# Third-block low parts of groups 0 to 2: VectorE in place of GpSimd, in an attention and two-MoE kernel

## The chip, the cores and the metric

The kernel runs on one NeuronCore of a Trainium2 chip. The metric is the device time of one execution in microseconds (us), the median of several runs. Engines are called by the names of the profile: PE is TensorE's matrix multiply and PEld its weight load, DVE is VectorE, ACT is ScalarE, POOL is GpSimd, SP is the queue that issues the transfers.

## The reference

All arithmetic is on 32-bit floats. Three layers follow one another; the output of each is the input of the next.

```
attention: q, k, v of 2 x 8 heads x 768 tokens x 64; a local band of 16 tokens plus 24 block summaries,
           softmax, product with v; the result is x with 1536 tokens x 512
layer 1:   h = x @ w_in (512 x 2048);  g = h * sigmoid(1.702 h);  x = g @ w_out (2048 x 512)
layer 2:   gate = sigmoid(x @ w_gate);  val = x @ w_val (both 512 x 1536);  out = (gate * val) @ w_out (1536 x 512)
```

## The kernel before, in words

**Products in high and low parts.** PE multiplies numbers of a shorter format (`F32R`). To keep the accuracy of 32 bits, every operand x is split into a high part xH, a rounded copy that ACT makes, and a low part xL = x - xH. A product is then three matmuls that add up in one PSUM bank: low times high, high times low, high times high (`mm3`, line 484, and `product`, line 190). A matmul of 128 x 512 streams 512 columns.

**Blocks and groups.** The 1536 tokens are three blocks (`blk` 0, 1, 2) of 512. The hidden features of a layer are cut into groups `g` of 256 (8 in layer 1, 6 in layer 2), a group into two tiles `f` of 128 features. `first` (line 517) computes the two feature tiles of one group and block: for each, 12 matmuls into a bank `ps_h`, then `gated`. `gated` (line 511) takes the activation with ACT into a tile `sg` and calls `split`. `split` (line 503) makes the high part `gh` with ACT (line 508) and the low part `gl` = `sg` - `gh` with GpSimd (line 509). `second` (line 541) multiplies the two tiles of a group by the group's rows of the output weights: four column pieces `m`, each 6 matmuls into a bank `ps_o`. Of group 0, ACT copies the piece into the accumulator `acc` (line 571); of later groups, DVE adds it (line 575). Within a piece the second matmul is the first to read `gl` of tile 0, and the fifth reads `gl` of tile 1.

**The stretch of the change.** Groups 0 and 1 of blocks 0 and 1 are done during the attention stage. Behind it, `steps` (line 925) lists three steps for the third block: groups 0, 1 and 2 (`PAIRED` is 2). The loop at line 927 gives PE this order: first of group 0, first of group 1, second of group 0, first of group 2, second of group 1. The second of group 2 is spread between the first products of the next phase. `run` (line 910) traces these; after each yield of the main generator it pulls one step of the weight loader (`load`, line 118) and one step of `folding`. From the second step on, `folding` is `input_sums` (line 248): thirteen DVE instructions on 128 x 1024 tiles (line 253), all with two inputs in SBUF, that form the sums and differences of blocks 0 and 1 and their low parts. The paired phase of group 2 onward (`pair`, line 402) needs these sums: it computes two feature tiles of two blocks with 7 products in place of 8. `load` brings one weight matrix piece of 128 x 1024 numbers: the DMA lands 64-bit words in `raw` (two buffers), DVE takes them apart (lines 132 and 150), ACT rescales (line 140) and rounds (line 155), DVE makes the low part (line 157). For some pieces it makes four sums as well (lines 173, 182, 184).

**What sets the order.** Only SP follows the program text by hand. On the other engines the order of instructions is fixed at build time: the framework's scheduler plays the program on a timeline of its own and issues what is ready there, the earlier in the program first. An engine then runs its list in that order, and waits at an instruction whose inputs are not there. `keep_in_program_order` (lines 134 and 254) pins an instruction behind the DVE instruction traced just before it; `behind` (line 111) pins one behind another that is named. Line 153 pins line 150 of group 3's input weights behind the addition of piece 0 of group 1, third block (`added[1, 1, 2, 0]`).

**Buffers.** After the attention stage the feature tiles have 7 buffers `sg` and 5 each of `gh` and `gl`; `ps_f` has four PSUM banks and `ps_s` four.

The lines that the change and the steps of the prediction touch:

```
927    for step in steps:
929        run(first(*step))
932        if prev: ... run(second(*prev, False))
937        if step == (1, 0, 2): folding = sums_1

912    for n, _ in enumerate(main):
913        pull(1)
914        next(folding, None)
```

Of the kernel before, what the change touches and what calls it, by code (L numbers as in the profile page):

```python
# [14 lines left out]
ALU = mybir.AluOpType  # L15
# [14 lines left out]
def attention_moe_moe2_kernel(ctx: ExitStack, tc: tile.TileContext, ins: dict, out: bass.AP):  # L30
    nc = tc.nc
# [186 lines left out]
    PAIRED = 2  # L218
# [123 lines left out]
    def halves(g):  # L342
# [30 lines left out]
        def out(j, f, x):  # L373
            if f not in sg:
                sg[f] = sg_slots.tile([P, TB], F32, "sg")
            to = sg[f][:, (FIRST, SECOND)[j]]
            nc.scalar.activation(to, x[:, FIRST], AF.Sigmoid)
            nc.vector.tensor_tensor(out=to, in0=x[:, SECOND], in1=to, op=ALU.mult)
            done[f] = done.get(f, 0) + 1
            if done[f] == 2:  # L380
                split((2, g, 2, f), sg[f])
# [116 lines left out]
    def gate_by(to, val, sg):  # L498

        nc.vector.tensor_tensor(out=sg, in0=val, in1=sg, op=ALU.mult)  # L500
        split(to, sg)

    def split(to, sg):
        name = "_".join(map(str, to))
        gh = gh_slots.tile([P, TB], F32R, f"gh{name}")
        gl = gl_slots.tile([P, TB], F32R, f"gl{name}")
        gt[to] = gh, gl
        nc.scalar.copy(gh, sg)  # L508
        nc.gpsimd.tensor_tensor(out=gl, in0=sg, in1=gh, op=ALU.subtract)  # L509

    def gated(to, x):

        sg = sg_slots.tile([P, TB], F32, "sg")
        nc.scalar.activation(sg, x, AF.Gelu_apprx_sigmoid)
        split(to, sg)
# [90 lines left out]
    with tc.manual_schedule(engines={mybir.EngineType.SP}), ExitStack() as es:  # L606
# [192 lines left out]
        for _ in range(4):  # L799
# [28 lines left out]
            out=win, in_=win, pattern=[[0, NSLOT], [1, P - W0]], compare_op=ALU.is_gt, fill=NEG,  # L828
# [3 lines left out]
            out=win, in_=win, pattern=[[0, NSLOT], [-1, P - W0]], compare_op=ALU.is_gt, fill=NEG,  # L832
# [225 lines left out]
```

## Time and profile before

| | us |
|---|---|
| median of 3 runs (lowest to highest) | 625.32 (624.49 to 626.36) |
| the profiled execution, its own time | 624.76 |
| its span, first to last instruction | 623.0 |

What lies outside the span is 1.76 us. In the profile, a time such as 137.19 is microseconds from the start of the span. A row of the timeline has start, duration, engine, line, operation, the tiles written and read, their shapes, and in brackets the idle time of the engine before the row with what ended it. Rows of one engine can overlap by a little: the next instruction starts before the last has drained, so the spacing of the starts is what one instruction costs its engine. The busy shares of the whole execution are 96% for PE, 71% for DVE, 51% for ACT and 33% for POOL. The granted clock of TensorE is 1.00 at 2.4 GHz and 0.50 at 1.2 GHz.

### The profile page before, as it was taken

The numbers are of one execution on the slowest core, as the hardware profiler recorded it, in microseconds if no ns is written. First come the engines' busy times: TensorE is split into PE (matmuls) and PEld (weight loads), VectorE is DVE, ScalarE is ACT, GpSimd is POOL, SyncE is SP. The second block draws the span as 40 slices with busy tenths as digits, with TensorE's granted clock in tenths as the row PEclk, the third lists the DMA queues.
The fourth block names the chain that finished last, engine by engine and source line by source line (L and its number), as shares of the span: only waits on it lengthen the run. The fifth ranks groups of instructions, "written<-read, shape, count | busy, mean of one in ns | idle before, by whom it ended". The sixth has DMA issues, their size and how long they took to land.

```text
span 623.0 us, 8772 instructions
## 1 busy us (share of the span) xinstructions
PE 600.9 (96%) x3342; PEld 499.3 (80%) x3342; DVE 445.2 (71%) x662; ACT 316.1 (51%) x624; POOL 205.4 (33%) x164
## 2 busy tenths in 40 slices
PE   7798999986999999999999999999999999999997
PEld 4576887765888888888888888888898888898896
DVE  6799666492799875975559889677778668777434
ACT  4688657572465444545345567635345245344230
POOL 6796676255133222321332131021121222112030
PEclk9999999996999999999999999999999999999999
DMA  9998742012044121230202003412211212100014
GB/s 314 344 308 284 250 121 66 1 68 67 1 135 136 69 67 68 68 108 28 68 0 69 0 2 135 135 68 67 70 68 68 67 68 69 68 1 0 1 46 157
DMA packets 25161, 58.10 MB, mean 93 GB/s; under 512 B 1568, under 2 KB 1824, under 8 KB 25120
## 3 DMA queue, kind: packets, MB, share of 16 engines
q1 hardware_dynamic: 24400, 56.24, 27.8%
q10 hardware_dynamic: 720, 1.31, 0.6%
q8 instruction: 26, 0.43, 0.3%
q14 instruction: 15, 0.12, 0.1%
HBM read 53.08 MB, written 3.15 MB: 90 GB/s over the span
## 4 chain that ended last, share of the span: by engine, by line
PE 87%; DMA 8%; POOL 3%; DVE 2%; issue 0%; ACT 0%; SPq 0%; ACTq 0%; POOLq 0%
PE ps_o L489 37%; PE ps_y L197 16%; PE ps_x L197 11%; PE ps_v L197 11%; PE ps_h L197 4%; PE ps_h L489 4%; DMA xH<-in_moe_w_out 3%; DMA k<-in_k 3%; POOL gl L509 2%; DMA vt<-in_vt 2%; PE ps_s L710 2%; PE ps_x L762 1%; PE ps_p L743 1%; DMA q<-in_q 1%; PE ps_s L708 0%
## 5 line engine op out<-in xcount | busy, mean ns | idle before, releaser
L509 POOL TENSOR_TENSOR gl<-sg,gh 128x512 fp32r<-128x512 f32 x84 | 131.8, 1576 | 380.2 <-ACT gh L508 279.8
L575 DVE TENSOR_TENSOR acc<-ps_o,acc 128x512 f32<-128x512 f32 x143 | 96.4, 684 | 71.8 <-PE ps_o L489 71.7
L489 PE MATMUL ps_o<-gl,w_1H 128*128 128x512 f32 x192 | 76.3, 399 | 7.8 <-POOL gl L509 7.8
L489 PE MATMUL ps_o<-gh,w_1H 128*128 128x512 f32 x192 | 75.5, 394 | 0.0
L489 PE MATMUL ps_o<-gh,w_1L 128*128 128x512 f32 x192 | 72.3, 401 | 1.5 <-ACT gh L508 1.4
L508 ACT CAST gh<-sg 128x512 fp32r<-128x512 f32 x84 | 51.5, 621 | 33.6 <-DVE sg L500 25.1
L489 PE MATMUL ps_o<-w_2L,gh 128*128 128x512 f32 (+1 forms) x146 | 56.6, 388 | 0.0
L489 PE MATMUL ps_o<-w_2H,gh 128*128 128x512 f32 (+1 forms) x146 | 56.4, 386 | 0.0
L489 PE MATMUL ps_o<-w_2H,gl 128*128 128x512 f32 (+1 forms) x146 | 56.3, 389 | 0.1
L150 DVE SCALAR_TENSOR_TENSOR da<-da,db 128x1024 uint32<-128x1024 uint32 x34 | 46.2, 1358 | 9.9 <-ACT da L140 9.2
L489 PEld LDWEIGHTS ps_o<-gl,w_1H 128*128 128x128 f32 x192 | 36.7, 191 | 15.8 <-POOL gl L509 8.4
L140 ACT ACTIVATE da<-da 128x1024 f32<-128x1024 f32 x34 | 36.1, 1061 | 20.8 <-DVE da L132 18.8
L489 PEld LDWEIGHTS ps_o<-gh,w_1L 128*128 128x128 f32 x192 | 36.5, 191 | 9.6 <-ACT gh L508 2.0
L489 PEld LDWEIGHTS ps_o<-gh,w_1H 128*128 128x128 f32 x192 | 36.6, 191 | 7.5
L723 ACT ACTIVATE e<-ps_s,nm 128x128 f32<-128x128 f32 x96 | 34.2, 377 | 9.4 <-DVE nm L715 8.3
L699 POOL TENSOR_SCALAR kx<-k 128x384 f32<-128x384 f32 x24 | 32.0, 1335 | 19.1 <-DMA k<-in_k 8.5
L489 PEld LDWEIGHTS ps_o<-w_2H,gh 128*128 128x128 f32 x146 | 27.4, 188 | 5.7
L489 PEld LDWEIGHTS ps_o<-w_2H,gl 128*128 128x128 f32 x146 | 27.4, 188 | 5.2 <-DVE acc L575 0.3
L489 PEld LDWEIGHTS ps_o<-w_2L,gh 128*128 128x128 f32 x146 | 27.5, 188 | 5.0
L710 PE MATMUL ps_s<-kx,q 128*128 128x128 f32 x192 | 28.5, 296 | 3.1 <-POOL kx L699 1.7
L710 PEld LDWEIGHTS ps_s<-kx,q 128*128 128x128 f32 x192 | 25.8, 205 | 6.7 <-POOL kx L699 3.2
L132 DVE TENSOR_SCALAR db<-raw 128x1024 uint32<-128x1024 uint32 x33 | 28.9, 877 | 0.5
(244 smaller groups left out, 1493.0 us busy)
## 6 DMA issues: line engine op xcount, KB each, us to landing
raw<-in_moe_w_out SPq DMA_DIRECT2D x13, 1024.0 KB, 5.1
raw<-in_moe_w_in SPq DMA_DIRECT2D x8, 1024.0 KB, 7.5
raw<-in_moe_w_gate SPq DMA_DIRECT2D x6, 1024.0 KB, 5.0
raw<-in_moe_w_val SPq DMA_DIRECT2D x6, 1024.0 KB, 5.2
q<-in_q SPq DMA_DIRECT2D x20, 256.0 KB, 9.3
vwin<-in_v SPq DMA_DIRECT2D x6, 768.0 KB, 9.1
k<-in_k SPq DMA_DIRECT2D x8, 400.0 KB, 7.5
out<-acc SPq DMA_DIRECT2D x11, 256.0 KB, 2.0
```

The costliest lines, as they stand in the source:

```text
L132: ins = nc.vector.tensor_scalar(**x)
L140: nc.scalar.activation(af, af, AF.Prelu, scale=REBIAS, alpha=-2.0 ** 32)
L150: ins = nc.vector.scalar_tensor_tensor(out=a, in0=a, scalar=3, in1=b, op0=ALU.logical_shift_left, op1=ALU.bitwise_or)
L197: nc.tensor.matmul(ps, lhsT=a[x][:, kk, :], rhs=b[y][:, kk, :], start=start and i == 0, stop=i == n - 1, skip_group_check=True,)
L489: nc.tensor.matmul(ps, lhsT=a, rhs=b, start=i == 0, stop=i == n - 1)
L508: nc.scalar.copy(gh, sg)
L509: nc.gpsimd.tensor_tensor(out=gl, in0=sg, in1=gh, op=ALU.subtract)
L575: added[layer, g, blk, m] = nc.vector.tensor_tensor(out=a[:, m, :], in0=ps, in1=a[:, m, :], op=ALU.add)
L699: nc.gpsimd.tensor_scalar(out=to, in0=x, scalar1=scale, scalar2=None, op0=ALU.mult)
L710: nc.tensor.matmul(ps[:, j, :], lhsT=t[:, j, :], rhs=kt[:, j, :], start=False, stop=j == G - 1)
L723: nc.scalar.activation(e[:, j, :], s[:, j, :], AF.Exp, bias=nm[:, j:j + 1], accum_out=sm[:, j:j + 1])
L743: nc.tensor.transpose(ps[:, j, :], e[:, j, :], ident)
```

## The change

Of `split`, the low part is computed by DVE and not by GpSimd when the tile is of layer 1, of group 0, 1 or 2, and of the third token block. These are six tiles: two of each group. The other 78 low parts stay with GpSimd.

```
 def split(to, sg):
...
         nc.scalar.copy(gh, sg)
-        nc.gpsimd.tensor_tensor(out=gl, in0=sg, in1=gh, op=ALU.subtract)
+
+        engine = nc.vector if to[0] == 1 and to[1] <= PAIRED and to[2] == 2 else nc.gpsimd
+        engine.tensor_tensor(out=gl, in0=sg, in1=gh, op=ALU.subtract)
```

`to` is (layer, group, block, tile).

## Rows read from the trace of the kernel before

**Rows 1.** The page: the engines, busy time and instructions.

```profile
PE 600.9 (96%) x3342; PEld 499.3 (80%) x3342; DVE 445.2 (71%) x662; ACT 316.1 (51%) x624; POOL 205.4 (33%) x164
```

**Rows 2.** Stretches: busy of PE, PEld, DVE, ACT, POOL; granted clock, DMA share, GB/s.

```profile
137.19:145.07 7.88, 0.39 (x2) 0.00 (x1) 6.71 (x7) 2.72 (x4) 7.88 (x2) 0.67 0.12 42
...
145.07:150.24 5.17, 5.17 (x12) 4.07 (x13) 0.00 (x0) 0.00 (x0) 3.65 (x3) 0.51 0.64 199
...
165.00:175.00 10.00, 10.00 (x46) 8.27 (x45) 9.83 (x14) 5.31 (x8) 1.29 (x1) 1.00 0.08 11
150.24:360.00 209.76, 209.76 (x927) 173.70 (x926) 155.96 (x197) 103.23 (x153) 53.52 (x37) 1.00 0.19 61
360.00:618.00 258.00, 258.00 (x1374) 223.25 (x1373) 181.16 (x257) 117.07 (x185) 51.27 (x35) 1.00 0.19 63
```

**Rows 3.** The waits of PE: engine, line, releaser: us in total, times, longest.

```profile
PE ps_o L489 <- POOL gl L509: 7.8, 2, 7.5
PE ps_s L708 <- ACT e L723: 2.1, 2, 1.2
```

**Rows 4.** The chain that ended last, 126 to 160 us: start, us, what.

```profile
131.90 13.13 POOL gl L509
...
145.07 7.87 PE ps_o L489 x23
152.94 5.44 PE ps_h L489 x24
```

**Rows 5.** The timeline of PE around the wait, and two later starts.

```profile
137.19 0.39 PE L489 MATMUL ps_o<-gh,w_1L 128*128 128x512 f32 x1
145.07 0.79 PE L489 MATMUL ps_o<-gl,w_1H 128*128 128x512 f32 x1 [7.49 <-POOL gl L509]
...
158.21 0.39 PE L489 MATMUL ps_o<-gh,w_1L 128*128 128x512 f32 x1
...
165.24 0.39 PE L489 MATMUL ps_o<-gl,w_1H 128*128 128x512 f32 x1
...
177.03 0.39 PE L197 MATMUL ps_h<-xH,w_0H 128*128 128x512 f32 x1
```

**Rows 6.** The timeline of ACT: the high parts of the six tiles.

```profile
131.20 0.62 ACT L508 CAST gh<-sg 128x512 fp32r<-128x512 f32 x1
...
133.39 0.61 ACT L508 CAST gh<-sg 128x512 fp32r<-128x512 f32 x1
...
138.43 0.62 ACT L508 CAST gh<-sg 128x512 fp32r<-128x512 f32 x1
...
159.10 0.62 ACT L508 CAST gh<-sg 128x512 fp32r<-128x512 f32 x1
```

**Rows 7.** Line 509 in the whole trace: ns shortest, median, longest.

```profile
L509 POOL TENSOR_TENSOR gl<-sg,gh x84: 1262/1295/13118, 56.4 to 612.9; 128x512 fp32r<-128x512 f32 x84
```

**Rows 8.** The timeline of DVE from 131 to 161 us, in part.

```profile
131.79 1.22 DVE L253 TENSOR_TENSOR f<-f,f 128x1024 f32<-128x1024 f32 x1
132.92 0.69 DVE L132 TENSOR_SCALAR db<-raw 128x1024 uint32<-128x1024 uint32 x1
...
143.21 0.69 DVE L132 TENSOR_SCALAR da<-raw 128x1024 f32<-128x1024 f32 x1
159.84 0.69 DVE L575 TENSOR_TENSOR acc<-ps_o,acc 128x512 f32<-128x512 f32 x1 [15.94 <-PE ps_o L489]
160.45 1.71 DVE L150 SCALAR_TENSOR_TENSOR da<-da,db 128x1024 uint32<-128x1024 uint32 x1
...
164.76 1.21 DVE L157 TENSOR_TENSOR w_0L<-da,w_0H 128x1024 fp32r<-128x1024 f32 x1
```

**Rows 9.** The timeline of POOL, 115 to 165 us.

```profile
131.90 16.82 POOL L509 TENSOR_TENSOR gl<-sg,gh 128x512 fp32r<-128x512 f32 x4 [10.88 <-ACT gh L508]
```

**Rows 10.** Line 582: a DVE subtraction with the operands of line 509.

```profile
L582 DVE TENSOR_TENSOR yL<-acc,yH x10: 406/680/1784, 324.5 to 359.7; 128x512 fp32r<-128x512 f32 x8, 128x256 fp32r<-128x256 f32 x2
```

**Rows 11.** The waits of DVE in the whole trace, the longest group.

```profile
DVE acc L575 <- PE ps_o L489: 71.7, 46, 15.9
```

## The prediction

> **What bounds the kernel now.** I read the page first: PE is busy for 96% of the span [rows 1]. The stretches say where: from 150.24 to 618 us PE is busy in every microsecond, at a granted clock of 1.00 [rows 2]. So from there on nothing but PE's own work sets the time, and what starts PE earlier ends the kernel earlier, as long as the other engines keep up. Then I read the waits of PE. They are few: 7.8 us for GpSimd's low part, in 2 waits, one of 7.5, and 2.1 us for the next group [rows 3]. The chain of work shows the one wait in its place: a single low part holds it from 131.90 for 13.13 us, and behind it PE's 23 matmuls take 7.87 us, where the 24 after that take 5.44 [rows 4]. The reader should see two losses: a stop, and slow matmuls after it.
>
> The timeline of PE names the stop. At 137.19 PE starts the second product of group 0, third block; its second matmul is the first to read the low part of tile 0 and starts at 145.07, after 7.49 us of idle time [rows 5]. The stretches show what it does to the clock: 0.67 in the stretch of the idle time, 0.51 from 145.07 to 150.24, that is the lower of the two levels (1.2 of 2.4 GHz), and 1.00 afterwards [rows 2].
>
> Why is a low part of 128 x 512 late by so much? Its high part is done at 131.20 + 0.62 = 131.82 [rows 6], and GpSimd starts 0.08 us later. The median of the 84 low parts is 1.295 us, the shortest 1.262; this one is the longest, 13.118 [rows 7]. Meanwhile DVE runs back to back: from the row at 131.79 to the end of the row at 143.21 its starts follow one another with no idle time in brackets, and then it stands for 15.94 us [rows 8]. DVE's last one ends at 143.21 + 0.69 = 143.90; GpSimd's ends at 131.90 + 13.13 = 145.03, which is 1.13 us later, a little less than one undisturbed low part. The other three, which waited in GpSimd's queue, take (16.82 - 13.13) / 3 = 1.23 us each once DVE stands [rows 4, 9]. So GpSimd got almost nothing done while DVE ran with operands in SBUF, and finished as soon as DVE stopped.
>
> **A rule against this reading.** The Trainium skill, SBUF — State Buffer, Who interferes with whom, says that a DVE instruction with two SBUF inputs and a GpSimd instruction that reads SBUF exclude each other, and that whoever issues first has the ports for that one instruction. By that rule GpSimd would wait for one DVE instruction, to 131.79 + 1.22 = 133.01, and be done at an estimated 134.3; the 7.49 us would have another cause. The trace agrees on the exclusion, and not on its length: the twelve DVE instructions from 131.79 to 143.21 all went first (the first two and the last of them stand in [rows 8]). I go by the trace; the other case is rival B.
>
> **The change, part by part.**
>
> *Removed: six low parts on GpSimd.* Four of them are the row of 16.82 us, two are later ones. Off PE's path but for the first.
>
> *Added: six on DVE.* The nearest row has the same operands, types and 512 columns: 0.68 us median [rows 10]. In a full queue one such instruction costs what lies between two starts, 160.45 - 159.84 = 0.61 us [rows 8], so 6 x 0.61 = 3.7 us of DVE time. DVE's list is fixed at build time, and no row shows the place of the six. They are early in the program, so each should stand about where its high part is done. The early end for tile 0 is 131.82 + 0.68 = 132.5. The late end is the last place ahead of the addition at 159.84, since PE makes that addition's input only after it has read the low part: 143.90 + 0.68 = 144.6. PE wants it at 137.42 (137.19 plus 0.23, the pitch of 5.44 / 24). I take the early end: even two places further, behind the rows at 131.79 and 132.92, it is done at 134.2. Tile 1 has its high part at 133.39 + 0.61 = 134.0 [rows 6] and, one DVE instruction of 1.22 later at worst, is done by 135.9; PE wants it at 137.19 + 4 x 0.23 = 138.1. Group 1's later high part is done at 138.43 + 0.62 = 139.05 [rows 6], and PE comes to group 1's low parts only after 48 more matmuls, past 148.
>
> *The sums behind them.* Four of the low parts push the rest of DVE's run back by 4 x 0.61 = 2.4 us, from 143.90 to 146.3. The cover is the 15.94 us in which DVE stands [rows 8]. It shrinks, as PE comes earlier (below): the addition then starts at 159.84 - 10.1 = 149.7, still 3.4 us behind 146.3. No DMA is issued or moved, and SP's own list stays.
>
> *The pins.* Each input sum is pinned behind the DVE instruction traced just before it. A low part could become that instruction, and the sums would stand behind it. In the code `run` pulls a loader step between the two, and where that step issues nothing on DVE, the addition of `second` has come in between. So I cost the pins at nothing.
>
> *The gain.* From 137.19 to 158.21, the start of the second product of group 1 [rows 5], PE has 48 matmuls: 24 of group 0's second and 24 of group 2's first. At 5.44 / 24 = 0.227 us [rows 4] they take 10.88; they took 21.02. The difference is 10.14 us: 145.07 - 137.19 - 0.23 = 7.65 for the stop and 2.49 for matmuls at the lower clock. I take it that the clock does not fall where PE does not stop: it is 1.00 throughout the 468 us from 150.24 on, in which PE never does [rows 2].
>
> *The last two low parts, and DVE after the gain.* Group 2's second high part is done at 159.72 [rows 6], by 149.6 after the change, and PE wants group 2's low part at 165.24 - 10.14 = 155.1 [rows 5]. Here DVE is nearly full: 9.83 of 10 us from 165 to 175 [rows 2]. The two cost 1.2 us; what GpSimd held up in return, the row at 160.45 with 1.71 against 1.22 for its size [rows 8], is 0.5. The end prices are 0 and +1.2 on PE's path. I take 0: the weights that DVE makes at 164.76 + 1.21 = 165.97 [rows 8] are read by PE at 177.03 at the earliest [rows 5], 11 us later, and all this moves forward with the addition that starts it.
>
> *Sum.* 624.76 - 10.1 + 0 = 614.6 for an execution like the profiled one. The median lies 0.56 above it, so 615.2.
>
> **The rivals.**
>
> *A. Partly given back.* DVE carries 3.7 us more, and in the full stretch after 165 PE has to wait once for a weight piece. Price: 3.7 of idle time and again 2.5 at the lower clock, 6.2 in all, so 621.4. For it: DVE at 9.83 of 10. Against: PE does not wait once from 150 on, and DVE waits for PE 46 times, for 71.7 us [rows 11].
>
> *B. The change does not do what it says.* Not DVE's traffic, but something else that a DVE instruction would meet as well, held the first low part; it then takes as long on DVE. Its end stays near 145.03, the sums behind it still fit ahead of 159.84, and the time is 625.3. Against: the three that follow it take 1.23 us.
>
> *C. Slower: the sums behind a low part that waits for PE.* If DVE's list has group 2's second low part ahead of the row at 131.79, DVE stands until its high part is done, at 149.6 at the best, and the 12.1 us of work up to 143.90 plus 3.7 follow: until 165.4. The first addition, wanted at 149.7, then lets its bank go only at about 166, and PE, out of banks at 154.9, stands for 11 us and pays 2.5 for the clock: 13.5 lost for 10.1 gained, 628.7. It decides as soon as more than about 9 us of that work stand behind. Against: the scheduler lets go ahead what is ready, and this one is ready last.
>
> **How the numbers follow.** The forecast has 0.84, A 0.08, B 0.05, C 0.03. A measurement of this kernel can tell 0.3%, 1.9 us, from no change. B is the same; the forecast and A lie beyond, so faster is 0.91, same 0.06 (B and a mild C), slower 0.03. The forecast's own range is 613.6 (the fastest run shown lies 0.8 below the median, and as much again for other small waits on GpSimd) to 617.0 (the 1.2 us of DVE on PE's path, and part of the clock). I reach up to 618.5, for low parts that stand a few places later, towards A; this leaves out most of A, B and C, under 0.2.
>
> **What would show it.** PE's wait for line 509 is gone from its waits, the row at 145.07 starts at 137.4, and 24 matmuls of that product take about 5.4 us at a clock of 1.00. The six DVE rows of line 509 take 0.68 us; DVE's wait for the addition is some 3 us in place of 15.94. No low part of GpSimd takes over 3 us. It is wrong if PE idles between 137 and 165 or waits for DVE rows later, if the clock still falls there, or if a DVE row of line 509 has idle time before it with sums behind.

## The result, and the profile after

The median of four runs is 615.69 us (615.31 to 616.76); the kernel before has 624.9 in four runs beside them. The ratio is 0.9851, with an interval of 0.983 to 0.9873. The profiled execution is the longest of the four: 616.76 us, span 615.0. The changed lines push the code behind them down by two: line 509 is 511 now, 575 is 577.

The page, the engines (answers to [rows 1]) and the shares of the chain:

```profile
PE 600.4 (98%) x3342; PEld 500.6 (81%) x3342; DVE 447.2 (73%) x668; ACT 316.5 (51%) x624; POOL 188.0 (31%) x158
...
PE 93%; DMA 4%; ACT 1%; DVE 1%; POOL 0%; issue 0%; SPq 0%; POOLq 0%
```

PE's work is what it was (600.9 us before). GpSimd's busy time fell by 17.4 us; the row of 16.82 [rows 9] is gone from it. Line 511 in the whole trace, as in [rows 7]:

```profile
L511 POOL TENSOR_TENSOR gl<-sg,gh x78: 1264/1296/2364, 58.2 to 604.9; 128x512 fp32r<-128x512 f32 x78
...
L511 DVE TENSOR_TENSOR gl<-sg,gh x6: 680/682/695, 135.1 to 153.5; 128x512 fp32r<-128x512 f32 x6
```

The low part of 13.118 us is gone, and no other has taken its place: GpSimd's longest takes 2.364. The waits of PE, the largest three; where [rows 3] had GpSimd's low part with 7.8 us, nothing of line 511 is left:

```profile
PE ps_s L712 <- DMA q<-in_q: 2.4, 2, 2.2
PE ps_s L710 <- ACT e L725: 1.8, 2, 0.9
PE ps_o L489 <- ACT gh L508: 1.7, 1, 1.7
```

All three are in the attention stage. The chain from 126 us on (compare [rows 4]), without the stop and without a slow stretch:

```profile
128.60 10.88 PE ps_h L489 x48
139.48 0.91 PE ps_o L489 x4
...
150.36 5.44 PE ps_o L489 x24
```

The stretches (columns as in [rows 2]) confirm it: the 21.76 us from the first product of the third block to the second product of group 1 are full, at a clock of 1.00.

```profile
128.44:139.32 10.88, 10.88 (x50) 9.01 (x48) 10.88 (x14) 7.57 (x10) 0.00 (x0) 1.00 0.14 44
139.32:150.20 10.88, 10.88 (x50) 9.01 (x48) 9.81 (x11) 7.39 (x11) 0.00 (x0) 1.00 0.18 61
150.20:360.00 209.80, 209.80 (x933) 173.77 (x932) 161.68 (x209) 104.37 (x154) 54.00 (x36) 1.00 0.20 65
```

**Two clocks to read by.** The first matmul of the third block starts at 128.44 here and started at 126.31 before. So every time of after is set against one of before plus 2.13. The *tail*, from that matmul to the end of the span, is 615.0 - 128.44 = 486.56; it was 623.0 - 126.31 = 496.69. The difference is 10.13 us; the spans are given to a tenth of a microsecond, so its last digit means little. The timeline of PE, from which these starts come (compare [rows 5]):

```profile
128.44 0.39 PE L489 MATMUL ps_h<-xH,w_0L 128*128 128x512 f32 x1
...
139.32 1.07 PE L489 MATMUL ps_o<-gh,w_1L 128*128 128x512 f32 x4
...
140.68 0.39 PE L489 MATMUL ps_o<-gl,w_1H 128*128 128x512 f32 x1
...
150.20 0.39 PE L489 MATMUL ps_o<-gh,w_1L 128*128 128x512 f32 x1
```

The build has changed the order of PE's list as well: six matmuls that do not read `gl` now stand ahead of the first one that does, at 140.68; before, it was one.

The timeline of DVE shows where the six stand (compare [rows 8]):

```profile
133.92 1.22 DVE L253 TENSOR_TENSOR f<-f,f 128x1024 f32<-128x1024 f32 x1
135.06 0.68 DVE L511 TENSOR_TENSOR gl<-sg,gh 128x512 fp32r<-128x512 f32 x1
...
137.40 0.68 DVE L511 TENSOR_TENSOR gl<-sg,gh 128x512 fp32r<-128x512 f32 x1
...
148.96 0.69 DVE L511 TENSOR_TENSOR gl<-sg,gh 128x512 fp32r<-128x512 f32 x1 [0.53 <-ACT gh L508]
151.76 0.69 DVE L577 TENSOR_TENSOR acc<-ps_o,acc 128x512 f32<-128x512 f32 x1 [2.10 <-PE ps_o L489]
153.50 0.69 DVE L511 TENSOR_TENSOR gl<-sg,gh 128x512 fp32r<-128x512 f32 x1
```

Four stand inside the run of the sums (two more at 141.41 and 144.88), which ends at 148.43; the fifth comes after it, the sixth between two additions. The 15.94 us in which DVE stood are now 0.53 and 2.10.

### The profile page after: what moved, and what is told of

It is laid out like the page before. It is cut to its first block, busy times and chain, and to the rows that moved or that the text cites. A ratio compares the mean times of both kernels' runs of the same rounds, so it can differ in the third digit from the quotient of the medians.

```text
span 615.0 us, 8762 instructions
## 1 busy us (share of the span) xinstructions
PE 600.4 (98%) x3342; PEld 500.6 (81%) x3342; DVE 447.2 (73%) x668; ACT 316.5 (51%) x624; POOL 188.0 (31%) x158
## 3 DMA queue, kind: packets, MB, share of 16 engines
q10 hardware_dynamic: 720, 1.31, 0.6%
## 4 chain that ended last, share of the span: by engine, by line
PE 93%; DMA 4%; ACT 1%; DVE 1%; POOL 0%; issue 0%; SPq 0%; POOLq 0%
PE ps_o L489 37%; PE ps_y L197 16%; PE ps_x L197 11%; PE ps_v L197 11%; PE ps_h L489 6%; PE ps_h L197 4%; PE ps_s L712 3%; DMA q<-in_q 3%; PE ps_x L764 2%; PE ps_p L745 2%; DMA k<-in_k 1%; PE ps_s L710 0%; ACT L524 0%; ACT e L725 0%; POOL kx L701 0%
## 5 line engine op out<-in xcount | busy, mean ns | idle before, releaser
L511 POOL TENSOR_TENSOR gl<-sg,gh 128x512 fp32r<-128x512 f32 x78 | 114.0, 1467 | 388.6 <-ACT gh L508 246.3
L701 POOL TENSOR_SCALAR kx<-k 128x384 f32<-128x384 f32 x24 | 33.5, 1396 | 18.2 <-PE ps_s L712 10.3
L712 PE MATMUL ps_s<-kx,q 128*128 128x128 f32 x192 | 30.9, 314 | 3.3 <-DMA q<-in_q 2.4
L712 PEld LDWEIGHTS ps_s<-kx,q 128*128 128x128 f32 x192 | 28.2, 222 | 6.4 <-DMA q<-in_q 2.3
```

The costliest lines, as they stand in the source:

```text
L511: engine.tensor_tensor(out=gl, in0=sg, in1=gh, op=ALU.subtract)
L701: nc.gpsimd.tensor_scalar(out=to, in0=x, scalar1=scale, scalar2=None, op0=ALU.mult)
L712: nc.tensor.matmul(ps[:, j, :], lhsT=t[:, j, :], rhs=kt[:, j, :], start=False, stop=j == G - 1)
```

## The experiments

The table sets the ten runs side by side; "start" is the first matmul of the third block in the run's profile, "tail" what follows it.

| run | which low parts, or what is added | median us | ratio [95%] | start | tail |
|---|---|---|---|---|---|
| (before) | none on DVE | 624.9 | 1 | 126.31 | 496.69 |
| e0_after | the change once more | 615.36 | 0.9848 [0.9834, 0.9861] | 127.05 | 486.45 |
| e1_group0 | group 0's two on DVE | 615.21 | 0.9842 [0.9828, 0.9855] | 126.68 | 486.52 |
| e2_groups12 | groups 1 and 2 on DVE | 626.0 | 1.0018 [1.0006, 1.003] | 126.69 | 498.11 |
| e3_tile0 | tile 0 of group 0 on DVE | 623.7 | 0.9974 [0.9964, 0.9985] | 126.22 | 494.58 |
| e5_pause | none; DVE waits for GpSimd | 616.35 | 0.9859 [0.9845, 0.9874] | 127.60 | 487.4 |
| e6_double | the six, each twice | 615.19 | 0.9841 [0.9826, 0.9856] | 126.89 | 486.51 |
| e7_all | all 84 on DVE | 617.19 | 0.9875 [0.9858, 0.9891] | 127.34 | 486.66 |
| e8_reduce | none; reductions on DVE | 616.08 | 0.9855 [0.9835, 0.9876] | 126.01 | 487.89 |
| e10_tiny | none; small reductions | 616.2 | 0.9872 [0.9847, 0.9896] | 126.91 | 487.4 |
| e9_scale | none; small multiplies | 616.53 | 0.9864 [0.9845, 0.9883] | 128.07 | 487.7 |

The kernel before had 624.75 to 625.06 beside them. The column of the starts moves by 2 us from profile to profile, also between two profiles of one kernel (128.44 and 127.05); the tails of the kernels that give both tiles of group 0 to DVE lie between 486.45 and 486.66. So the tail is the sharper measure of this change.

### Which of the six matter

**e0_after**, the change unedited, and **e1_group0**:

```
-  engine = nc.vector if to[0] == 1 and to[1] <= PAIRED and to[2] == 2 else nc.gpsimd
+  engine = nc.vector if to[:3] == (1, 0, 2) else nc.gpsimd
```

> The changed kernel again, for a second trace of its attention stage. If the attention stage differs only from run to run, the first matmul of the third block's first product lies somewhere between 125 and 129 us, the rest from there to the end is 486.5 us again, and the time is 615 to 616 us. If the change itself makes the stage longer, it starts near 128.4 again.

> Only the two low parts of group 0 go to DVE; those of groups 1 and 2 stay with GpSimd. Theory (only the first low part was waited for, the others have slack): GpSimd's low parts of group 1 are still held up until DVE's run of sums ends, for some 9 and 7 us, but PE wants them only at about 148.3 on the scale of before, so PE does not wait or waits under 1 us: 615 to 617 us. Rival (all six matter): PE waits for group 1's low part and the clock falls again, 618 to 622 us.

The repeat gives 615.36 and a tail of 486.45. With group 0's two alone the tail is 486.52: the whole gain. GpSimd still has a low part of some 10 us in e1 (line 509 there, as in [rows 7], then the timeline of GpSimd):

```profile
L509 POOL TENSOR_TENSOR gl<-sg,gh x82: 1271/1298/10023, 57.1 to 603.1; 128x512 fp32r<-128x512 f32 x82
```

```profile
136.60 12.52 POOL L509 TENSOR_TENSOR gl<-sg,gh 128x512 fp32r<-128x512 f32 x3 [15.21 <-ACT gh L508]
```

It ends at 136.60 + 10.02 = 146.62, which is 1.15 us after DVE's run (145.47), the same picture as before with 1.13. But it is group 1's, which PE reads only at 148.66, and no wait of PE comes of it. A low part held that long costs only where PE wants it sooner.

**e2_groups12**, the other four alone:

```
+  engine = nc.vector if to[:3] in ((1, 1, 2), (1, 2, 2)) else nc.gpsimd
```

> The reverse: group 0's two low parts stay with GpSimd, the four of groups 1 and 2 go to DVE. Theory: the stop is where it was, and DVE's run is longer by up to two low parts (1.2 us), so PE waits 7.5 to 8.7 us and the time is 625 to 627 us. Rival (GpSimd was late because four low parts queued on it): the wait shrinks by several us, 618 to 622 us.

626.0 us, no gain at all, and the tail is 1.4 us longer than before. The chain of e2:

```profile
132.28 14.33 POOL gl L509
...
146.66 8.11 PE ps_o L489 x23
```

Group 0's first low part, alone on GpSimd again, now takes 14.33 us in place of 13.13. Two of DVE's own low parts have come into the run (140.19 and 141.93), which makes it 2 x 0.61 = 1.2 us longer, and GpSimd is later by just that much (14.33 - 13.13 = 1.20). It ends at 146.61, the run at 145.48: again 1.13 us apart. So the end of the low part follows the end of DVE's run, not a length of its own.

**e3_tile0**, one tile:

```
+  engine = nc.vector if to == (1, 0, 2, 0) else nc.gpsimd
```

> Only tile 0 of group 0 goes to DVE. Theory (GpSimd gets nothing done while DVE runs back to back on SBUF): the low part of tile 1 is now the one that takes some 10 us, up to the end of DVE's run; PE stops at it, 3 matmuls later than before, and the time is 623 to 626 us. Rival (one DVE instruction at most goes first): tile 1's low part takes under 2.6 us, PE does not wait, 615 to 617 us.

Tile 1 takes the place of tile 0: its low part takes 11.55 us and ends 1.13 us behind DVE's run (145.54 against 144.41). The wait in the timeline of PE, and the stretches of the stop and behind it:

```profile
145.59 0.79 PE L489 MATMUL ps_o<-gl,w_1H 128*128 128x512 f32 x1 [5.83 <-POOL gl L509]
```

```profile
139.36:145.59 6.23, 0.40 (x3) 0.01 (x1) 5.05 (x5) 0.70 (x1) 6.23 (x2) 0.79 0.02 3
145.59:149.90 4.31, 4.31 (x11) 3.40 (x11) 0.00 (x0) 1.17 (x2) 2.41 (x2) 0.52 0.75 239
```

The stop is 5.83 us: eleven matmuls of PE's list stand between the start of the second product (137.10) and the stop, where the expectation had four. The clock falls again: 0.79 in the stop, 0.52 behind it. This stop, of another tile and another length, has the same two losses as that of before. One tile gains a fifth of what two gain (2.1 of 10.1 us of tail).

### Is it DVE's run that holds GpSimd?

**e5_pause** leaves all low parts on GpSimd and makes DVE read one column of each as soon as it is done, four times:

```
+  pause = const.tile([P, 1], F32, name="pause")
...
   nc.gpsimd.tensor_tensor(out=gl, in0=sg, in1=gh, op=ALU.subtract)
+  if to[:3] in ((1, 0, 2), (1, 1, 2)):
+      nc.vector.tensor_copy(pause, gl[:, 0:1].bitcast(F32))
```

> All low parts stay with GpSimd, as before; DVE copies one column of each low part of groups 0 and 1 (third block), so that it stops at each copy until GpSimd has finished. Theory (GpSimd only needs DVE to stop): DVE stops near 133.5 us, and the low part of tile 0 ends some 1.2 us later, so it takes 2 to 4 us instead of 13; PE does not wait; DVE loses 4 times about 1.2 us, which its idle time before the first addition still covers: 615 to 617 us. Rival (GpSimd itself is slow there, or the gain needs the low parts on DVE): 623 to 627 us.

616.35 us, and PE no longer waits for a low part. GpSimd's first one starts at 133.19 and takes 2.88. The timeline of DVE:

```profile
136.10 0.15 DVE L512 COPY pause<-gl 128x1 f32<-128x1 f32 x1 [1.20 <-POOL gl L510]
```

DVE stands for 1.20 us, and in that time GpSimd does its instruction. Nothing else of GpSimd's work was touched, so a low part is not slow by itself, and not held by ACT or a transfer: DVE's unbroken run held it. That refutes rival B. The price is in DVE's sums, which take 2.22 to 2.31 us where GpSimd is first, in place of 1.22. The tail is 487.4, some 0.9 longer than the change's; 0.6 us of that is PE waiting once for an addition.

**e8_reduce** puts three reductions of each high part of group 0 on DVE. They read one tile, and read or write nothing else of the computation:

```
+  if to[:3] == (1, 0, 2):
+      for _ in range(3):
+          nc.vector.tensor_reduce(out=pause, in_=gh.bitcast(F32), axis=AX.X, op=ALU.max)
```

> All low parts on GpSimd; between the sums DVE does six reductions with one SBUF input, three on each high part of group 0, about 0.65 us each, three of them between 132 and 140 us. By the rule of the ports (only a DVE instruction with two SBUF inputs or in a 2-port mode keeps GpSimd out) GpSimd works during the reductions: its low part of tile 0 needs two of them and ends at 134 to 140 us, and PE waits 0 to 3 us: 615 to 620 us. Rival (GpSimd must find DVE idle): the low part ends 1.1 us after DVE's run, which is 2 to 4 us longer than before; it takes 15 to 17 us, and the time is 626 to 629 us.

616.08 us, the median of two runs, and a tail of 487.89. DVE never stands for GpSimd here by a semaphore, and yet GpSimd's first low part takes 2.27 us in place of 13.12. The timeline of DVE (a line was added ahead of these, so 133 was 132 and 254 was 253):

```profile
132.63 0.68 DVE L513 TENSOR_REDUCE pause<-gh 128x1 f32<-128x512 f32 x1
133.23 1.19 DVE L133 TENSOR_SCALAR db<-raw 128x1024 uint32<-128x1024 uint32 x1
134.34 2.31 DVE L254 TENSOR_TENSOR f<-f,f 128x1024 f32<-128x1024 f32 x1
```

GpSimd's low part, issued at 131.60, ends at 133.87: that is 132.63, the start of the reduction, plus 1.24, one undisturbed low part. DVE's next instruction takes 1.19 in place of 0.69 [rows 8]: it has to wait until GpSimd is done. GpSimd was waiting at three reductions of e8 (132.63, 136.57 and 141.08), and each time it got in. So a reduction, which has a single input in SBUF, lets GpSimd in. The Trainium skill, SBUF — State Buffer, Who interferes with whom, has a reduction never in conflict with GpSimd on this chip, and a `tensor_scalar` able to take both port pairs. The trace agrees on the reduction. It fits the other as well: line 132 does 1024 columns in 0.69 us, line 253 needs 1.22 [rows 8], and neither let the first low part in before.

**e10_tiny** is e8_reduce with the reductions cut to 64 columns:

```
-          nc.vector.tensor_reduce(out=pause, in_=gh.bitcast(F32), axis=AX.X, op=ALU.max)
+          nc.vector.tensor_reduce(out=pause, in_=gh[:, 0:64].bitcast(F32), axis=AX.X, op=ALU.max)
```

> As the kernel with reductions, but each of the six reads only 64 columns of the high part, about 0.2 us. Theory (GpSimd takes the ports at the start of any DVE instruction that leaves them free, and keeps them for its own whole instruction): the low part of tile 0 ends 1.3 us after the first reduction starts, so takes 2 to 3 us, and the DVE instruction behind the reduction is 1 us longer; 615 to 617 us. Rival (the free time has to be long enough for GpSimd's instruction, or a good part of it): the low part still takes over 10 us, 624 to 627 us.

```profile
133.53 0.21 DVE L513 TENSOR_REDUCE pause<-gh 128x1 f32<-128x64 f32 x1
133.66 1.66 DVE L133 TENSOR_SCALAR db<-raw 128x1024 uint32<-128x1024 uint32 x1
```

In this timeline of DVE 0.21 us of a reduction are enough. GpSimd starts at 132.50, gets in at 133.53 and ends at 134.76, while DVE's next instruction takes 1.66 us, 0.97 more than its 0.69. GpSimd needs an opening, not a pause as long as its own instruction: once in, it keeps DVE out until it is done. The tail is 487.4, as with the pause; the median is 616.2.

A reduction is not the only thing that lets GpSimd in. A later low part of e10 got in straight ahead of a sum with two inputs, behind another such (the timelines of GpSimd and of DVE):

```profile
139.29 1.81 POOL L510 TENSOR_TENSOR gl<-sg,gh 128x512 fp32r<-128x512 f32 x1 [2.82 <-issue]
```

```profile
138.74 1.21 DVE L254 TENSOR_TENSOR t1L<-f,t1H 128x1024 fp32r<-128x1024 f32 x1
139.87 2.31 DVE L254 TENSOR_TENSOR f<-f,f 128x1024 f32<-128x1024 f32 x1
```

The low part ends at 141.10, one undisturbed low part after 139.87, and the sum takes 2.31 us in place of 1.22. In the timeline of DVE of before, the same two sums kept GpSimd out:

```profile
135.80 1.22 DVE L253 TENSOR_TENSOR t1L<-f,t1H 128x1024 fp32r<-128x1024 f32 x1
136.93 1.22 DVE L253 TENSOR_TENSOR f<-f,f 128x1024 f32<-128x1024 f32 x1
```

The same happened in e5 (the sum at 140.59) and in e8 (the sum at 146.80). So sums with two inputs do not always keep GpSimd out; what makes the difference is open. Not one of the twelve instructions of before let it in, nor did DVE's runs in e1, e2 and e3.

**e9_scale** puts a multiply by one in the place of these reductions, on 64 columns too, an operation of the kind of line 132:

```
+          nc.vector.tensor_scalar(out=pause, in0=gh[:, 0:64].bitcast(F32), scalar1=1.0, scalar2=None, op0=ALU.mult)
```

> The same six places, with a multiplication by one of 64 columns from SBUF to SBUF in place of the reduction, the kind of line 132, which has one input but ran in the blocking run of before. Theory (this kind keeps GpSimd out as the ones with two inputs do): nothing opens, the low part of tile 0 takes 13 to 15 us and PE waits 7.5 to 9 us: 624 to 627 us. Rival (one input in SBUF is what opens the ports, or any further instruction): the low part takes 2 to 3 us, 615 to 617 us.

The first two low parts take 4.14 and 4.67 us: neither of the two forecasts, and PE waits only 0.88 us for one of them. The timeline of DVE:

```profile
134.69 0.19 DVE L513 TENSOR_SCALAR pause<-gh 128x64 f32<-128x64 f32 x1
...
136.53 1.32 DVE L513 TENSOR_SCALAR pause<-gh 128x64 f32<-128x64 f32 x1
```

The first multiply did not let GpSimd in (0.19 us); at the second one GpSimd went first and DVE waited 1.1 us. The later ones (141.18 and 145.28) took 1.30 and 1.31 as well. This settles nothing: the same operation went both ways. Which instructions with one input let GpSimd in stays open; shown is the reduction, five times of five (two of them in e10, at 133.53 and 142.11).

### Is DVE short of time?

**e6_double** computes each of the six twice on DVE; **e7_all** gives all 84 low parts to DVE:

```
+  if to[0] == 1 and to[1] <= PAIRED and to[2] == 2:
+      nc.vector.tensor_tensor(out=gl, in0=sg, in1=gh, op=ALU.subtract)
```

```
-  nc.gpsimd.tensor_tensor(out=gl, in0=sg, in1=gh, op=ALU.subtract)
+  nc.vector.tensor_tensor(out=gl, in0=sg, in1=gh, op=ALU.subtract)
```

> The change, with each of the six low parts computed twice on DVE, 3.7 us more DVE time. Theory (DVE's extra time lies in its idle time and PE does not want its products): within 1 us of the changed kernel, 615 to 616.5 us, DVE's wait before the first addition down to nothing. Rival A of the prediction (DVE is nearly full and PE comes to wait for it): 617 to 622 us, with PE waits for DVE rows after 150 us.

> All 84 low parts on DVE. In the changed kernel PE waits for none of the other 78, so nothing is to be had; DVE gets 78 times 0.61, 48 us, more over the span, in stretches that are 90% full. Theory: no gain, 615.5 to 620 us, with some PE waits for DVE rows. Rival (GpSimd and DVE hold each other up everywhere, which costs PE too): 610 to 614.5 us.

e6 has another 3.7 us of DVE's time in that stretch, and e7 moves the other 78 as well. The tails are 486.51 and 486.66, those of the change. In e6 the build put some matmuls of group 0's second product later, and the first addition comes at 155.65. So DVE's wait before it is not down to nothing, as was expected, but 3.95 us; PE waits for nothing there. The page of each, the engines:

```profile
PE 599.3 (98%) x3342; PEld 498.5 (81%) x3342; DVE 451.7 (74%) x674; ACT 316.0 (52%) x624; POOL 186.2 (30%) x158
```

```profile
PE 598.6 (97%) x3342; PEld 499.1 (81%) x3342; DVE 465.8 (76%) x746; ACT 318.3 (52%) x624; POOL 74.4 (12%) x80
```

With 465.8 us of work DVE still does not hold PE behind the attention stage: the profile of e7 has no wait of PE there, where some had been expected. e7's median is 1.8 us above the change's repeat, and its tail only 0.2. Where the rest lies is not shown, since the one profile is of its fastest run (615.82). Ahead of the third block e7 has low parts on DVE too.

## Why the prediction was right

The prediction was 615.2 us, the medians are 615.69 and 615.36. Its mechanism is what the trace and the runs show: DVE's run held one low part, PE stopped for it and went on at the lower clock, and both losses are gone.

*The gain.* Forecast 10.14 us, from the 48 matmuls that took 21.02. The tail fell by 10.13, and the distance from the first product of the third block to the second of group 1 by 31.90 - 21.76 = 10.14. The first matmul to read the low part, at 145.07 in [rows 5], was to come at 137.42, which is 139.55 in after's time. PE has no idle time there, but by the build's new order it runs other matmuls first and comes to this one at 140.68. The gain does not hang on that order: the low part is done by 135.74, and in e5, e8 and e10 the second matmul reads it, as before, without a stop. The clock term is in it: 1.00 throughout, and e3 shows that a stop brings the clock down again.

*Cause.* DVE's back-to-back run held GpSimd. The prediction had this from the ends alone (1.13 us apart). In e1, e2 and e3 the longest low part ends 1.15, 1.13 and 1.13 us behind the run, wherever that ends; e5, e8 and e10 take the hold away with the low part still on GpSimd. So rival B is refuted. The rule that GpSimd waits for one instruction of DVE failed for the first low part, which waited for twelve. It held for later ones, as at 139.87 in e10. When GpSimd has got in, DVE waits once, for up to about a microsecond.

*Where the six stand.* The early end for tile 0 was taken, 132.5, or 134.63 in after's time. It is done at 135.06 + 0.68 = 135.74, one place behind its high part, inside the margin of two places. PE comes to it 4.9 us later.

*The sums behind them.* They were to end at 146.3, which is 148.43 in after's time; they end at 148.43. The first addition was to start at 149.7 (151.8 in after's time), and starts at 151.76. The cover of 3.4 us is there, but the fifth low part stands in it: 0.53 and 2.10 of idle time remain, together 2.63 where the forecast was some 3.

*The pins, and the last two low parts.* Both were taken at nothing, and 10.13 of 10.14 us leave them nothing. For the latter, with bounds of 0 and 1.2, e6 is the stronger evidence: twice the work there, and no wait of PE.

*Rivals A and C.* A, DVE as the next limit, would have to show in e6 and e7, and does not. C needed group 2's second low part ahead of the run of sums: it stands behind it, at 153.50. But one sign by which the prediction was to be wrong did show: the fifth low part, at 148.96, has 0.53 us of idle time before it, and the sums at 154.70 and 158.84 stand behind. It costs nothing, since DVE waits another 2.10 us for PE after it. The sign was set too sharp.

*What the prediction had too large by a little.* The median fell by 9.2 and, in the repeat, by 9.5 us, not by 10.1. The forecast time came out closer than that, since its kernel before, at 625.32, was itself 0.4 above the 624.9 measured beside the result: the two errors went against each other, which is luck. The step is the last one of the sum, which takes everything ahead of the change as it was. The attention stage ends later in after's profile by 2.13 and in e0's by 0.74. The waits of PE ahead of 126 us show a possible cause for a part of it, a load of q (the waits of e0 have none of it); one row of before and one of after:

```profile
PE ps_s L710 <- DMA q<-in_q: 1.3, 1, 1.3
```

```profile
PE ps_s L712 <- DMA q<-in_q: 2.4, 2, 2.2
```

The instructions there have the same order in both kernels. Of before there is one profile, and e3, e2 and e8 with starts of 126.22, 126.69 and 126.01 lie on both sides of it. Whether a few tenths of it are systematic was not settled.

## What to carry to other kernels

Compare the longest duration of a group with its median. Here a GpSimd instruction ten times as long as its like stood beside an unbroken run of DVE, and ended about one undisturbed duration after that run did, so look for such a run. If PE wants its result soon, give it to DVE itself, where it costs the spacing of two starts (0.61 us here against up to 14.3); only the low parts with a near deadline have to move. A stop of DVE or a short reduction in its run let GpSimd in too, but left the kernel some 0.9 us longer (e5, e10). A stop of PE costs more than its length where the clock falls behind it, so a stop of 7.65 us was worth 10.14.

## What the runs showed of the hardware that had not been expected

An instruction of 0.21 us on DVE, a reduction with one input, cut a low part on GpSimd from 13.12 to 2.26 us. Once GpSimd is in, DVE's next instruction waits for it: in e5, e8, e9 and e10 that one is longer by 0.5 to 1.13 us. How long GpSimd waits is not a fixed rule: in before, twelve instructions of DVE in a row went first, and in e10 a later low part got in ahead of a sum that had kept it out in before. The starts within DVE's run are closer together than its instructions are long (1.13 against 1.22, from 131.79 and 132.92 in [rows 8]), which could mean that the ports never come free between two of them. But the two sums of e10 start 1.13 us apart as well, so this alone does not explain the hold.

Behind the stretch GpSimd is never held for long (2.364 us is its longest low part in after), though DVE is busy there too. The timelines of GpSimd and DVE in the kernel after show a likely reason:

```profile
166.09 2.29 POOL L511 TENSOR_TENSOR gl<-sg,gh 128x512 fp32r<-128x512 f32 x1 [42.94 <-DVE acc L577]
```

```profile
167.13 0.68 DVE L577 TENSOR_TENSOR acc<-ps_o,acc 128x512 f32<-128x512 f32 x1
167.73 1.20 DVE L132 TENSOR_SCALAR db<-raw 128x1024 uint32<-128x1024 uint32 x1
```

The low part ends at 168.38, that is 1.25 us after the start of an addition that reads one input from a PSUM bank and only one from SBUF, and DVE's next instruction takes 1.20 in place of 0.69. Of the 27 low parts of after that took over 1.4 us, 13 end 1.2 to 1.3 us after the start of such an addition. The run that held GpSimd in before has none. This was read from the trace; no run took the additions away. The multiply of e9, which let GpSimd in only at its second place, is not explained by any of this.
